# A fused hash attention and MoE kernel: score windows of one PSUM bank in a rotation of three, two output accumulators, a new plan and start fillers

## The chip, the cores and the metric

One core of a Trainium2 chip. The metric is the device time of one execution in microseconds (us). Times are medians over several executions; the span of a profile is 1.5 to 2 us less. The kernel before runs in 360 us.

PE is TensorE's matmuls and PEld its weight loads; ACT is ScalarE, DVE is VectorE, POOL is GpSimd. PSUM is the memory into which matmuls write. AV is the product of the exps of the scores with V. MoE is the name of the two last matmuls of the reference, with h * sigmoid(h) between them.

## The reference, cut to what matters

```python
def _attn_ref(q, k, v, proj):            # q, k, v: 4 x 8 x 768 x 64
    q_bits = (np.einsum('bhsd,dk->bhsk', q, proj) > 0)   # 6 bits; k_bits alike
    mask = q_bucket[:, :, :, None] == k_bucket[:, :, None, :]
    scores = np.where(mask, scale * np.matmul(q, k.transpose(0, 1, 3, 2)), -1e9)
    attn = softmax(scores)               # written out in the original
    return np.matmul(attn, v)

x = attn_out.transpose(0, 2, 1, 3).reshape(B * S, H * D)   # 3072 x 512
h = x @ w_in                             # 512 x 2048
return (h * sigmoid(h)) @ w_out          # 2048 x 512
```

There are 32 heads. A block of 768 rows of x needs all eight heads of its batch, so the MoE of batch b runs between the heads of batch b + 1. The first batch has no MoE work beside it, and the MoE of the last batch runs alone at the end.

## The kernel before

PSUM has eight banks. The general pool `m` has three, the scores `s` four (two tiles of 768 columns, each over two banks), the accumulator `o` one.

```python
def score(s):                            # one key tile of a head
    sp = ps.tile([P, S], F32, tag="s", name="s_ps", bufs=2)
    ks = t[rows, S + jt * P : S + (jt + 1) * P]
    for c0, c1 in ((0, 512), (512, S)):
        nc.tensor.matmul(sp[:, c0:c1], ks, t[rows, c0:c1], start=True, stop=True)
    u = upl.tile([P, S], F16, tag="u", name="u")
    nc.scalar.activation(out=u, in_=sp, func=AF.Exp, scale=ESC)

def av(s):
    if jt == 0:                          # a new head: start the accumulator
        o_ps[h] = ps.tile([P, NJ, E1], F32, tag="o", name="o_ps", bufs=1)
        nc.tensor.matmul(o_ps[h], dmat, vs[...].to_broadcast(...), start=True, stop=True)
    for t in range(NJ):                  # six matmuls of 65 columns
        nc.tensor.matmul(o_ps[h][:, t, :], u[:, t * P : (t + 1) * P], vv[:, jt, :], ...)
    if jt == NJ - 1:                     # head done: normalise on VectorE
        nc.vector.reciprocal(out=rec, in_=o[:, :, D])
        nc.vector.tensor_tensor(out=x_pr[p][...], in0=o[:, :, 0:D], in1=rec..., op=ALU.mult)
# ...
for s in range(NSTEP):
    for fn in at.pop(s, []): fn()        # planned units
    # ... n MoE units from the queue
    av(s)
    if s + 2 < NSTEP: score(s + 2)
```

The planned units are: `t_unit` (four f32 transposes of q or k, and a copy from PSUM), `cast_unit` (POOL, f16 copies of q and k), `proj_unit` (the six hash bits by matmul), `bits_unit` (VectorE writes bits below q and k, so that the score matmul masks by itself), `v_unit` (POOL) and `x_unit` (transpose of the normalised output).

The softmax here doesn't subtract the row's maximum and nothing guards it: scores larger than these inputs give would overflow.

Of the kernel before, what the change touches and what calls it, by code (L numbers as in the profile page):

```python
# [9 lines left out]
F32 = mybir.dt.float32  # L10
F16 = mybir.dt.float16
# [6 lines left out]
def kernel(  # L18
# [10 lines left out]
    nc = tc.nc  # L29
# [19 lines left out]
    vld = ctx.enter_context(tc.tile_pool(name="vld", bufs=4))  # L49
    t32 = ctx.enter_context(tc.tile_pool(name="t32", bufs=4))  # L50
    btp = ctx.enter_context(tc.tile_pool(name="btp", bufs=2))
    upl = ctx.enter_context(tc.tile_pool(name="upl", bufs=4))
    nrm = ctx.enter_context(tc.tile_pool(name="nrm", bufs=2))
    xpl = ctx.enter_context(tc.tile_pool(name="xpl", bufs=2))
    thp = ctx.enter_context(tc.tile_pool(name="thp", bufs=3))
# [10 lines left out]
    def load_qk(p):  # L66
        b, h0 = p // 4, 2 * (p % 4)
        for n, src in (("q", q), ("k", k)):
            t = ld.tile([P, NJ, 2, D], F32, tag=f"ld{n}", name=f"{n}_sb")
            nc.sync.dma_start(  # L70
                out=t, in_=src[b, h0 : h0 + 2].rearrange("h (p t) d -> p t h d", p=P))
            qk_sb[p, n] = t
# [15 lines left out]
    nc.vector.memset(dmat, DELTA)  # L88
    warm = cst.tile([P, 512], BF16, name="warm")
    nc.vector.memset(warm, 0.5)  # L90
    wps = ps.tile([P, 512], F32, tag="o", name="warm_ps", bufs=1)

    def warm_up(n):
        for _ in range(n):
# [47 lines left out]
    def load_w_in(dt):  # L142
        nc.gpsimd.dma_start(out=w_in16[dt], in_=moe_w_in[P * dt : P * (dt + 1), :])
# [9 lines left out]
    def t_unit(p, i, warm=0):  # L153
        if i == 0:
            qk32[p] = t32.tile([P, 2 * S], F32, tag="qk32", name="qk32")
        tp = ps.tile([P, 512], F32, tag="m", name="tp_ps", bufs=3)
        for j in range(4):
            n, t = divmod(4 * i + j, NJ)
            src = qk_sb[p, "qk"[n]]
            if t == 0 and n == 1:  # L160
                warm_up(warm)
            nc.tensor.transpose(tp[:, j * P : (j + 1) * P],  # L162
                                src[:, t].rearrange("p h d -> p (h d)"), ident)
        dst = qk32[p][:, 512 * i : 512 * (i + 1)]
        if p > 3 or p == 0 and i != 1:
            nc.scalar.copy(dst, tp)  # L166
        else:
            nc.vector.tensor_copy(out=dst, in_=tp)

    def cast_unit(p, par):  # L170
        sl = p % NSL
        dst, rows = ((QKA[sl], slice(0, 64)), (QKB[sl], slice(64, 128)))[par]
        nc.gpsimd.tensor_scalar(out=dst[rows, :], in0=qk32[p][rows, :],  # L173
                                scalar1=CS, scalar2=1.0,
                                op0=ALU.mult, op1=ALU.mult)

    def v_unit(p, heads=(0, 1)):
        for i in heads:
            h = 2 * p + i
            vv, vs = VV[h % NVS], VS[h % NVS]  # L180
            src = v_sb[p][:, i, :].rearrange("p (t d) -> p t d", d=D)
            nc.gpsimd.tensor_copy(out=vv[:, :, 0:D], in_=src)
            sa = nrm.tile([P, 3, D], F32, tag="vsa", name="vsa")
            nc.gpsimd.tensor_tensor(out=sa, in0=src[:, 0:3], in1=src[:, 3:6], op=ALU.add)  # L184
            sb = nrm.tile([P, D], F32, tag="vsb", name="vsb")
            nc.gpsimd.tensor_tensor(out=sb, in0=sa[:, 0], in1=sa[:, 1], op=ALU.add)
            nc.gpsimd.tensor_tensor(out=vs[:, 0:D], in0=sb, in1=sa[:, 2], op=ALU.add)
# [33 lines left out]
                nc.vector.tensor_copy(out=dst, in_=bits[pairs][r, :])  # L221


    st = {}
    ut = {}

    def score(s):
        h, jt = divmod(s, NJ)
        p, par = divmod(h, 2)
        t = QKA[p % NSL] if par == 0 else QKB[p % NSL]  # L230
        rows = slice(0, 65 + NBIT) if par == 0 else slice(0, P)
        sp = ps.tile([P, S], F32, tag="s", name="s_ps", bufs=2)
        ks = t[rows, S + jt * P : S + (jt + 1) * P]
        for c0, c1 in ((0, 512), (512, S)):
            nc.tensor.matmul(sp[:, c0:c1], ks, t[rows, c0:c1], start=True, stop=True)  # L235
        u = upl.tile([P, S], F16, tag="u", name="u")
        nc.scalar.activation(out=u, in_=sp, func=AF.Exp, scale=ESC)  # L237
        ut[s] = u

    o_ps = {}  # L240
    x_pr = {}

    def av(s):
        h, jt = divmod(s, NJ)
        vv, vs = VV[h % NVS], VS[h % NVS]
        if jt == 0:
            o_ps[h] = ps.tile([P, NJ, E1], F32, tag="o", name="o_ps", bufs=1)
            nc.tensor.matmul(o_ps[h], dmat, vs[:, None, :].to_broadcast([P, NJ, E1]),  # L248
                             start=True, stop=True)
        u = ut.pop(s)  # L250
        for t in range(NJ):
            nc.tensor.matmul(o_ps[h][:, t, :], u[:, t * P : (t + 1) * P], vv[:, jt, :],  # L252
                             start=False, stop=True,
                             skip_group_check=True)
        if jt == NJ - 1:
            o = o_ps.pop(h)
            p, par = divmod(h, 2)
            if par == 0:
                x_pr[p] = xpl.tile([P, NJ, P], F16, tag="xpr", name="x_pr")
            rec = nrm.tile([P, NJ], F32, tag="rec", name="rec")  # L260
            nc.vector.reciprocal(out=rec, in_=o[:, :, D])  # L261
            nc.vector.tensor_tensor(out=x_pr[p][:, :, par * D : (par + 1) * D],  # L262
                                    in0=o[:, :, 0:D],
                                    in1=rec[:, :, None].to_broadcast([P, NJ, D]),
                                    op=ALU.mult)
# [58 lines left out]


    NH = B * H
    NSTEP = NH * NJ
    QST = 4 * NJ

    t_unit(0, 0)  # L330
    t_unit(0, 1, warm=6)
    t_unit(0, 2)
    cast_unit(0, 0)
    v_unit(0, (0,))
    proj_unit(0)
    bits_unit((0,), 0, 0)
    cast_unit(0, 1)
    v_unit(0, (1,))
    bits_unit((0,), 0, 1)

    at = {}

    def plan(step, fn):
        at.setdefault(step, []).append(fn)


    for i in range(3):
        plan(1 + i, lambda i=i: t_unit(1, i))
    plan(3, lambda: cast_unit(1, 0))
    plan(3, lambda: cast_unit(1, 1))  # L350
    plan(5, lambda: proj_unit(1))
    plan(5, lambda: bits_unit((1,), 0, 0))
    plan(6, lambda: bits_unit((1,), 0, 1))
    plan(6, lambda: v_unit(1))
    for i in range(2):
        plan(0, lambda p=2 + i: load_qk(p))
    for i in range(2):
        plan(2 + i, lambda p=2 + i: load_v(p))

    for i in range(6):  # L360
        plan(8 + 2 * i, lambda i=i: t_unit(2 + i // 3, i % 3))
        if i % 3 == 2:
            for par in range(2):
                plan(8 + 2 * i, lambda p=2 + i // 3, par=par: cast_unit(p, par))
    plan(19, lambda: proj_unit(2, 3))
    for i in range(4):
        plan(19 + i, lambda i=i: bits_unit((2, 3), i // 2, i % 2))
    for i in range(2):
        plan(14 + i, lambda p=2 + i: v_unit(p))
    for dt in range(NDT):  # L370
        plan(8 + 4 * dt, lambda dt=dt: load_w_in(dt))
        plan(25 + 4 * dt, lambda dt=dt: load_w_out(dt))
    for i in range(2):
        plan(14 + i, lambda p=4 + i: load_qk(p))

    for Q in range(2, NQUAD):
        s0 = (Q - 1) * QST
        for i in range(6):
            plan(s0 + 2 * i, lambda Q=Q, i=i: t_unit(2 * Q + i // 3, i % 3))
            if i % 3 == 2:  # L380
                for par in range(2):
                    plan(s0 + 2 * i, lambda p=2 * Q + i // 3, par=par: cast_unit(p, par))
        plan(s0 + 13, lambda Q=Q: proj_unit(2 * Q, 2 * Q + 1))
        for i in range(4):
            plan(s0 + 14 + i,
                 lambda Q=Q, i=i: bits_unit((2 * Q, 2 * Q + 1), i // 2, i % 2))
        for i in range(2):
            plan(s0 + 1 + i, lambda p=2 * Q + i: load_v(p))
            plan(s0 + 16 + i, lambda p=2 * Q + i: v_unit(p))
            if Q + 1 < NQUAD:  # L390
                plan(s0 + 12 + i, lambda p=2 * Q + 2 + i: load_qk(p))
    for p in range(NPAIR):
        plan(12 * (p + 1) + 2, lambda p=p: x_unit(p))

    moeq = deque()
    score(0)
    score(1)
    for s in range(NSTEP):
        for fn in at.pop(s, []):
            fn()  # L400
        if s % 48 == 3 and s > 48:
            moeq.extend(moe_units(s // 48 - 1))
        keep = 3 if s >= NSTEP - 8 else 0
        left = 48 - s % 48
        n = -(-(len(moeq) - keep) // left) if len(moeq) > keep else 0
        for _ in range(n):
            moeq.popleft()()
        av(s)
        if s + 2 < NSTEP:
            score(s + 2)  # L410
    while moeq:
        moeq.popleft()()
    for s in sorted(at):
        for fn in at[s]:
            fn()
    for u in moe_units(B - 1):
        u()


# [1 line left out]
_INS = ['q', 'k', 'v', 'proj', 'moe_w_in', 'moe_w_out']  # L421
# [26 lines left out]
```

## Time and profile before

The span, cut at the first exp, at the first MoE matmul of three batches, and at the last AV matmuls (the prediction cuts up to 0.4 us elsewhere). Each busy time is of the stretch; the last column is the mean granted clock. This profile is of an execution of 361.78 us with a recorded clock of 0.976, which the record counts as slow. No fast execution of this kernel was profiled.

| stretch | us | PE busy | ACT busy | clock |
|---|---|---|---|---|
| start | 13.15 | 9.35 | 2.46 | 1.00 |
| first batch, attention alone | 62.3 | 52.9 | 43.5 | 0.86 |
| mixed 1, attention and MoE | 81.8 | 77.9 | 57.2 | 1.00 |
| mixed 2 | 81.8 | 77.9 | 57.1 | 1.00 |
| mixed 3 | 72.1 | 67.6 | 50.5 | 1.00 |
| MoE alone | 48.9 | 45.0 | 14.3 | 1.00 |

In the views below, a wait line names who waited, `<-` for whom, then us in total, times, and the longest. A line of the timeline gives start, us, engine, source line, operation, tiles, shapes and count; in brackets, the idle time just before and who ended it. Ends of matmuls are modelled.

Two lines of the page are of use beside those that the prediction shows: the granted clock in 40 slices of 9 us, in tenths, and the matmul that starts an accumulator, with busy time, mean ns, then idle before it and who ended most of that.

```profile
PEclk9789989699999999999999999999999999999999
L248 PE MATMUL o_ps<-vs,dmat 128*128 128x390 f16 x32 | 10.9, 341 | 19.0 <-DVE x_pr L262 16.8
```

The clock falls in the first 75 us alone. PE stood still for 19.0 us ahead of 32 short matmuls, 16.8 of it until a normalisation had read the one accumulator.

### The profile page before, as it was taken

The numbers are of one execution on the slowest core, as the hardware profiler recorded it, in microseconds if no ns is written. First come the engines' busy times: TensorE is split into PE (matmuls) and PEld (weight loads), VectorE is DVE, ScalarE is ACT, GpSimd is POOL, SyncE is SP. The second block draws the span as 40 slices with busy tenths as digits, with TensorE's granted clock in tenths as the row PEclk, the third lists the DMA queues.
The fourth block names the chain that finished last, engine by engine and source line by source line (L and its number), as shares of the span: only waits on it lengthen the run. The fifth ranks groups of instructions, "written<-read, shape, count | busy, mean of one in ns | idle before, by whom it ended". The sixth has DMA issues, their size and how long they took to land.

```text
span 360.0 us, 7115 instructions
## 1 busy us (share of the span) xinstructions
PE 330.6 (92%) x2893; PEld 195.7 (54%) x2893; DVE 162.4 (45%) x335; ACT 225.0 (63%) x327; POOL 111.9 (31%) x178
## 2 busy tenths in 40 slices
PE   7779798699989999999989999999989999999995
PEld 4446364365467664565457664555457555446542
DVE  4555615344584216245594116235584222277421
ACT  2348688598678664688678564588778465366200
POOL 5766968411820228002730229003640000000000
PEclk9789989699999999999999999999999999999999
DMA  8999999900000008397000009230000001000012
GB/s 185 237 240 251 237 183 219 231 6 0 2 2 1 31 29 182 84 213 169 2 0 3 29 31 188 76 118 2 1 3 0 31 31 58 32 29 2 29 60 87
DMA packets 60257, 29.83 MB, mean 83 GB/s; under 512 B 50496, under 2 KB 56640, under 8 KB 60224
## 3 DMA queue, kind: packets, MB, share of 16 engines
q1 hardware_dynamic: 57472, 25.17, 29.5%
q0 software_dynamic: 2752, 4.20, 6.7%
q8 instruction: 23, 0.38, 0.5%
q14 instruction: 10, 0.08, 0.1%
HBM read 27.27 MB, written 6.29 MB: 93 GB/s over the span
## 4 chain that ended last, share of the span: by engine, by line
PE 71%; DVE 16%; ACT 4%; issue 3%; POOL 3%; DMA 1%; ACTq 0%; POOLq 0%
PE o_ps L306 22%; PE h_ps L289 18%; PE s_ps L235 13%; PE o_ps L252 8%; DVE g L295 5%; PE tp_ps L162 4%; DVE x_pr L262 4%; PE bp_ps L201 3%; PE o_ps L248 3%; DVE qka L221 2%; ACT th L293 2%; ACT u L237 2%; DVE osb L311 1%; DVE qkb L218 1%; DMA q_sb<-in_q_dram 1%
## 5 line engine op out<-in xcount | busy, mean ns | idle before, releaser
L237 ACT ACTIVATE u<-s_ps 128x768 f16<-128x768 f32 x192 | 153.9, 812 | 82.7 <-PE s_ps L235 81.9
L306 PE MATMUL o_ps<-wout,g 128*128 128x512 f16 x384 | 94.5, 379 | 0.0
L289 PE MATMUL h_ps<-xT,win 128*128 128x512 f16 (+1 forms) x512 | 93.8, 326 | 0.3 <-DVE xT L274 0.3
L295 DVE SCALAR_TENSOR_TENSOR g<-th,h_ps 128x512 f16<-128x512 f32 x96 | 66.0, 687 | 49.5 <-ACT th L293 49.2
L252 PEld LDWEIGHTS <-u 128*128 128x128 f16 x1152 | 59.9, 100 | 40.0 <-ACT u L237 13.2
L252 PE MATMUL o_ps<-vv,u 128*128 128x65 f16 x1152 | 68.5, 197 | 2.6 <-ACT u L237 2.0
L293 ACT ACTIVATE th<-h_ps 128x512 f32<-128x512 f32 x96 | 57.3, 597 | 21.8 <-PE h_ps L289 19.2
L173 POOL TENSOR_SCALAR qka<-qk 64x1536 f16<-64x1536 f32 x16 | 23.4, 1462 | 145.3 <-ACT qk L166 137.6
L289 PEld LDWEIGHTS <-win 128*128 128x128 f16 x512 | 49.5, 98 | 31.1 <-issue 1.8
L306 PEld LDWEIGHTS <-g 128*128 128x128 f16 x384 | 37.0, 98 | 36.3 <-issue 0.8
L235 PE MATMUL s_ps<-qka 71*128 71x512 f16 x192 | 48.9, 337 | 1.9 <-DVE qka L221 1.9
L235 PE MATMUL s_ps<-qkb 128*128 128x512 f16 x192 | 48.2, 333 | 0.0
L311 DVE TENSOR_SCALAR osb<-o_ps 128x512 f32<-128x512 f32 x24 | 16.6, 692 | 63.9 <-PE o_ps L306 63.9
L248 PE MATMUL o_ps<-vs,dmat 128*128 128x390 f16 x32 | 10.9, 341 | 19.0 <-DVE x_pr L262 16.8
L166 ACT COPY qk<-tp_ps 128x512 f32<-128x512 f32 x38 | 22.2, 584 | 6.0 <-PE tp_ps L162 6.0
L173 POOL TENSOR_SCALAR qkb<-qk 64x1536 f16<-64x1536 f32 x16 | 23.5, 1469 | 1.3
L274 DVE COPY xT<-xt_ps 128x768 f16<-128x768 f16 x16 | 8.9, 556 | 23.1 <-PE xt_ps L272 23.0
L184 POOL TENSOR_TENSOR vsa<-v_sb 128x192 f32<-128x192 f32 x32 | 19.3, 604 | 0.0
L248 PEld LDWEIGHTS <-dmat 128*128 128x128 bf16 x32 | 3.1, 96 | 29.3 <-issue 14.9
L261 DVE RECIPROCAL rec<-o_ps 128x6 f32<-128x6 f32 x32 | 6.1, 190 | 27.7 <-PE o_ps L252 27.6
L262 DVE TENSOR_TENSOR x_pr<-o_ps,rec 128x384 f16<-128x384 f32 x32 | 17.8, 557 | 1.1
L206 DVE TENSOR_SCALAR bits<-bp_ps,sc 128x512 f16<-128x512 f32 (+3 forms) x18 | 11.3, 671 | 14.7 <-PE bp_ps L201 14.7
(43 smaller groups left out, 212.4 us busy)
## 6 DMA issues: line engine op xcount, KB each, us to landing
q_sb<-in_q_dram SPq DMA_DIRECT2D x16, 384.0 KB, 7.1
k_sb<-in_k_dram SPq DMA_DIRECT2D x16, 384.0 KB, 7.0
v_sb<-in_v_dram SPq DMA_DIRECT2D x16, 384.0 KB, 5.5
out_dram<-osb SPq DMA_DIRECT2D x24, 256.0 KB, 2.0
win<-in_moe_w_in_dram POOLq DMA_DIRECT2D x4, 512.0 KB, 6.9
wout<-in_moe_w_out_dram POOLq DMA_DIRECT2D x4, 512.0 KB, 10.1
pw<-in_proj_dram POOLq DMA_DIRECT2D x2, 1.5 KB, 4.6
```

Of the source, the lines that this page charges most:

```text
L166: nc.scalar.copy(dst, tp)
L173: nc.gpsimd.tensor_scalar(out=dst[rows, :], in0=qk32[p][rows, :], scalar1=CS, scalar2=1.0, op0=ALU.mult, op1=ALU.mult)
L235: nc.tensor.matmul(sp[:, c0:c1], ks, t[rows, c0:c1], start=True, stop=True)
L237: nc.scalar.activation(out=u, in_=sp, func=AF.Exp, scale=ESC)
L248: nc.tensor.matmul(o_ps[h], dmat, vs[:, None, :].to_broadcast([P, NJ, E1]), start=True, stop=True)
L252: nc.tensor.matmul(o_ps[h][:, t, :], u[:, t * P : (t + 1) * P], vv[:, jt, :], start=False, stop=True, skip_group_check=True)
L262: nc.vector.tensor_tensor(out=x_pr[p][:, :, par * D : (par + 1) * D], in0=o[:, :, 0:D], in1=rec[:, :, None].to_broadcast([P, NJ, D]), op=A ...
L289: nc.tensor.matmul(hp[:, j, :], w_in16[dt][:, ft * P : (ft + 1) * P], xT[4 * b + dt][:, c0 : c0 + n], start=(dt == 0), stop=(dt == NDT - 1))
L293: nc.scalar.activation(out=th, in_=hp, func=AF.Tanh, scale=0.5)
L295: nc.vector.scalar_tensor_tensor(out=g[ci][:, grp * f : (grp + 1) * f, :], in0=th, scalar=1.0, in1=hp, op0=ALU.add, op1=ALU.mult)
L306: nc.tensor.matmul(o2[tt], g[ci][:, ft, ct * P : (ct + 1) * P], w_out16[:, ft, :], start=(ft == 0), stop=(ft == NFT - 1))
L311: nc.vector.tensor_scalar(out=osb, in0=o2[tt], scalar1=0.5, scalar2=None, op0=ALU.mult)
```

## The change

The same matmul columns, cut otherwise: a head has nine score windows of 512 columns (the middle one of three holds the 256-column rests of two key tiles), each in one bank. Three of them rotate, and the bank that this frees is a second accumulator. The plan is rewritten in windows, with the projections behind a head's end; the start has more filler matmuls and a cast on ScalarE in place of POOL.

```diff
+    LEAD = 3
-        sp = ps.tile([P, S], F32, tag="s", name="s_ps", bufs=2)
+        sp = ps.tile([P, 512], F32, tag="s", name="s_ps", bufs=LEAD)
-        for c0, c1 in ((0, 512), (512, S)):
-            nc.tensor.matmul(sp[:, c0:c1], ks, t[rows, c0:c1], start=True, stop=True)
+        for jt, c0, n, o0 in pts:
+            nc.tensor.matmul(sp[:, o0 : o0 + n], t[rows, S + jt * P : S + (jt + 1) * P],
+                             t[rows, c0 : c0 + n], start=True, stop=True)
-            o_ps[h] = ps.tile([P, NJ, E1], F32, tag="o", name="o_ps", bufs=1)
+            o_ps[h] = ps.tile([P, NJ, E1], F32, tag="o", name="o_ps", bufs=2)
 ...
-    t_unit(0, 1, warm=6)
+    t_unit(0, 1, warm=4)
     t_unit(0, 2)
+    warm_up(3)
     cast_unit(0, 0)
-    v_unit(0, (0,))
+    cast_unit(0, 1)
+    v_unit(0)
     proj_unit(0)
+    warm_up(9)
 ...
-    plan(5, lambda: proj_unit(1))
+    plan(9, lambda: proj_unit(1))
 ...
-        plan(s0 + 13, lambda Q=Q: proj_unit(2 * Q, 2 * Q + 1))
+        plan(w0 + 19, lambda Q=Q: proj_unit(2 * Q, 2 * Q + 1))
 ...
-        if s + 2 < NSTEP:
-            score(s + 2)
+        if w + LEAD < NW:
+            score(w + LEAD)
```

MoE units go into the first two of three windows. The SBUF pool of the exps goes from four tiles of 768 columns to six of 512, which are the same columns. The rest of the diff converts step numbers to window numbers.

More of the change, by code (lines that the diff above doesn't have):

```diff
@@ L51 @@
     btp = ctx.enter_context(tc.tile_pool(name="btp", bufs=2))
-    upl = ctx.enter_context(tc.tile_pool(name="upl", bufs=4))
+    upl = ctx.enter_context(tc.tile_pool(name="upl", bufs=6))
     nrm = ctx.enter_context(tc.tile_pool(name="nrm", bufs=2))
@@ L90 @@
     nc.vector.memset(warm, 0.5)
-    wps = ps.tile([P, 512], F32, tag="o", name="warm_ps", bufs=1)
+    wps = ps.tile([P, 512], F32, tag="o", name="warm_ps", bufs=2)
     def warm_up(n):
@@ L172, in cast_unit @@
         dst, rows = ((QKA[sl], slice(0, 64)), (QKB[sl], slice(64, 128)))[par]
+        if p == 0 and par == 1:
+            nc.scalar.mul(dst[rows, :], qk32[p][rows, :], CS)
+            return
         nc.gpsimd.tensor_scalar(out=dst[rows, :], in0=qk32[p][rows, :],
@@ L221, in bits_unit, with parts, score @@
                 nc.vector.tensor_copy(out=dst, in_=bits[pairs][r, :])
-    st = {}
+    NU = 9
+    LEAD = 3
     ut = {}
-    def score(s):
-        h, jt = divmod(s, NJ)
+    def parts(w):
+        h, r = divmod(w, NU)
+        jp, j = divmod(r, 3)
+        if j == 1:
+            return h, [(2 * jp, 512, 256, 0), (2 * jp + 1, 512, 256, 256)]
+        return h, [(2 * jp + j // 2, 0, 512, 0)]
+    def score(w):
+        h, pts = parts(w)
         p, par = divmod(h, 2)
@@ L231, in score, with av @@
         rows = slice(0, 65 + NBIT) if par == 0 else slice(0, P)
-        sp = ps.tile([P, S], F32, tag="s", name="s_ps", bufs=2)
-        ks = t[rows, S + jt * P : S + (jt + 1) * P]
-        for c0, c1 in ((0, 512), (512, S)):
-            nc.tensor.matmul(sp[:, c0:c1], ks, t[rows, c0:c1], start=True, stop=True)
-        u = upl.tile([P, S], F16, tag="u", name="u")
+        sp = ps.tile([P, 512], F32, tag="s", name="s_ps", bufs=LEAD)
+        for jt, c0, n, o0 in pts:
+            nc.tensor.matmul(sp[:, o0 : o0 + n], t[rows, S + jt * P : S + (jt + 1) * P],
+                             t[rows, c0 : c0 + n], start=True, stop=True)
+        u = upl.tile([P, 512], F16, tag="u", name="u")
         nc.scalar.activation(out=u, in_=sp, func=AF.Exp, scale=ESC)
-        ut[s] = u
+        ut[w] = u
     o_ps = {}
     x_pr = {}
-    def av(s):
-        h, jt = divmod(s, NJ)
+    def av(w):
+        h, pts = parts(w)
         vv, vs = VV[h % NVS], VS[h % NVS]
-        if jt == 0:
-            o_ps[h] = ps.tile([P, NJ, E1], F32, tag="o", name="o_ps", bufs=1)
+        if w % NU == 0:
+            o_ps[h] = ps.tile([P, NJ, E1], F32, tag="o", name="o_ps", bufs=2)
             nc.tensor.matmul(o_ps[h], dmat, vs[:, None, :].to_broadcast([P, NJ, E1]),
                              start=True, stop=True)
-        u = ut.pop(s)
-        for t in range(NJ):
-            nc.tensor.matmul(o_ps[h][:, t, :], u[:, t * P : (t + 1) * P], vv[:, jt, :],
-                             start=False, stop=True,
-                             skip_group_check=True)
-        if jt == NJ - 1:
+        u = ut.pop(w)
+        for jt, c0, n, o0 in pts:
+            for i in range(n // P):
+                nc.tensor.matmul(o_ps[h][:, c0 // P + i, :],
+                                 u[:, o0 + i * P : o0 + (i + 1) * P], vv[:, jt, :],
+                                 start=False, stop=True, skip_group_check=True)
+        if w % NU == NU - 1:
             o = o_ps.pop(h)
@@ L326, with plan @@
     NH = B * H
-    NSTEP = NH * NJ
-    QST = 4 * NJ
+    NW = NH * NU
+    BST = 8 * NU
+    QST = 4 * NU
     t_unit(0, 0)
-    t_unit(0, 1, warm=6)
+    t_unit(0, 1, warm=4)
     t_unit(0, 2)
+    warm_up(3)
     cast_unit(0, 0)
-    v_unit(0, (0,))
+    cast_unit(0, 1)
+    v_unit(0)
     proj_unit(0)
+    warm_up(9)
     bits_unit((0,), 0, 0)
-    cast_unit(0, 1)
-    v_unit(0, (1,))
     bits_unit((0,), 0, 1)
     at = {}
-    def plan(step, fn):
-        at.setdefault(step, []).append(fn)
+    def plan(w, fn):
+        at.setdefault(w, []).append(fn)
@@ L347 @@
     for i in range(3):
-        plan(1 + i, lambda i=i: t_unit(1, i))
-    plan(3, lambda: cast_unit(1, 0))
-    plan(3, lambda: cast_unit(1, 1))
-    plan(5, lambda: proj_unit(1))
-    plan(5, lambda: bits_unit((1,), 0, 0))
-    plan(6, lambda: bits_unit((1,), 0, 1))
-    plan(6, lambda: v_unit(1))
+        plan(1 + 2 * i, lambda i=i: t_unit(1, i))
+    plan(5, lambda: cast_unit(1, 0))
+    plan(5, lambda: cast_unit(1, 1))
+    plan(9, lambda: proj_unit(1))
+    plan(9, lambda: v_unit(1))
     for i in range(2):
+        plan(10 + i, lambda i=i: bits_unit((1,), 0, i))
@@ L356 @@
         plan(0, lambda p=2 + i: load_qk(p))
-    for i in range(2):
-        plan(2 + i, lambda p=2 + i: load_v(p))
+        plan(3 + i, lambda p=2 + i: load_v(p))
     for i in range(6):
-        plan(8 + 2 * i, lambda i=i: t_unit(2 + i // 3, i % 3))
+        plan(12 + 3 * i, lambda i=i: t_unit(2 + i // 3, i % 3))
         if i % 3 == 2:
             for par in range(2):
-                plan(8 + 2 * i, lambda p=2 + i // 3, par=par: cast_unit(p, par))
-    plan(19, lambda: proj_unit(2, 3))
+                plan(12 + 3 * i, lambda p=2 + i // 3, par=par: cast_unit(p, par))
@@ L366 @@
+    plan(28, lambda: proj_unit(2, 3))
     for i in range(4):
-        plan(19 + i, lambda i=i: bits_unit((2, 3), i // 2, i % 2))
+        plan(29 + i, lambda i=i: bits_unit((2, 3), i // 2, i % 2))
     for i in range(2):
-        plan(14 + i, lambda p=2 + i: v_unit(p))
+        plan(21 + i, lambda p=2 + i: v_unit(p))
+        plan(21 + i, lambda p=4 + i: load_qk(p))
     for dt in range(NDT):
-        plan(8 + 4 * dt, lambda dt=dt: load_w_in(dt))
-        plan(25 + 4 * dt, lambda dt=dt: load_w_out(dt))
@@ L373 @@
-    for i in range(2):
-        plan(14 + i, lambda p=4 + i: load_qk(p))
+        plan(12 + 6 * dt, lambda dt=dt: load_w_in(dt))
+        plan(38 + 6 * dt, lambda dt=dt: load_w_out(dt))
     for Q in range(2, NQUAD):
-        s0 = (Q - 1) * QST
+        w0 = (Q - 1) * QST
         for i in range(6):
-            plan(s0 + 2 * i, lambda Q=Q, i=i: t_unit(2 * Q + i // 3, i % 3))
+            plan(w0 + 3 * i, lambda Q=Q, i=i: t_unit(2 * Q + i // 3, i % 3))
             if i % 3 == 2:
                 for par in range(2):
-                    plan(s0 + 2 * i, lambda p=2 * Q + i // 3, par=par: cast_unit(p, par))
-        plan(s0 + 13, lambda Q=Q: proj_unit(2 * Q, 2 * Q + 1))
+                    plan(w0 + 3 * i, lambda p=2 * Q + i // 3, par=par: cast_unit(p, par))
@@ L384 @@
+        plan(w0 + 19, lambda Q=Q: proj_unit(2 * Q, 2 * Q + 1))
         for i in range(4):
-            plan(s0 + 14 + i,
+            plan(w0 + 20 + i,
                  lambda Q=Q, i=i: bits_unit((2 * Q, 2 * Q + 1), i // 2, i % 2))
         for i in range(2):
-            plan(s0 + 1 + i, lambda p=2 * Q + i: load_v(p))
-            plan(s0 + 16 + i, lambda p=2 * Q + i: v_unit(p))
+            plan(w0 + 1 + i, lambda p=2 * Q + i: load_v(p))
+            plan(w0 + 24 + i, lambda p=2 * Q + i: v_unit(p))
@@ L390 @@
             if Q + 1 < NQUAD:
-                plan(s0 + 12 + i, lambda p=2 * Q + 2 + i: load_qk(p))
+                plan(w0 + 18 + i, lambda p=2 * Q + 2 + i: load_qk(p))
     for p in range(NPAIR):
-        plan(12 * (p + 1) + 2, lambda p=p: x_unit(p))
+        plan(2 * NU * (p + 1) + 3, lambda p=p: x_unit(p))
     moeq = deque()
-    score(0)
-    score(1)
-    for s in range(NSTEP):
-        for fn in at.pop(s, []):
-            fn()
-        if s % 48 == 3 and s > 48:
-            moeq.extend(moe_units(s // 48 - 1))
-        keep = 3 if s >= NSTEP - 8 else 0
-        left = 48 - s % 48
+    for w in range(LEAD):
+        score(w)
@@ L405 @@
+    for w in range(NW):
+        for fn in at.pop(w, []):
+            fn()
+        if w % BST == 4 and w > BST:
+            moeq.extend(moe_units(w // BST - 1))
+        keep = 3 if w >= NW - 12 else 0
+        left = BST - w % BST
         n = -(-(len(moeq) - keep) // left) if len(moeq) > keep else 0
+        if w % 3 == 2 and n == 1 and len(moeq) - keep < left:
+            n = 0
         for _ in range(n):
             moeq.popleft()()
-        av(s)
-        if s + 2 < NSTEP:
-            score(s + 2)
+        av(w)
+        if w + LEAD < NW:
+            score(w + LEAD)
@@ L411 @@
     while moeq:
         moeq.popleft()()
-    for s in sorted(at):
-        for fn in at[s]:
+    for w in sorted(at):
+        for fn in at[w]:
             fn()
```

## The prediction

> **What bounds the kernel now.** I read the page's busy table first (PE 92% busy, ACT 63%), then cut the span at the first exp (13.15 us), the starts of the MoE matmuls of the first three batches (75.6, 157.4, 239.2) and the last attention step (311.5). The view of these stretches, with busy time of PE, PEld, DVE, ACT, POOL, then the clock, DMA share and GB/s:
>
> ```profile
> 0.00:13.15 13.15, 9.35 (x36) 4.41 (x37) 6.53 (x50) 2.46 (x3) 8.25 (x16) 1.00 1.01 208
> 13.15:75.60 62.45, 53.02 (x552) 32.19 (x551) 28.68 (x56) 43.66 (x60) 40.15 (x63) 0.86 1.08 214
> 75.60:157.40 81.80, 77.92 (x722) 47.63 (x720) 37.07 (x71) 57.17 (x85) 25.41 (x40) 1.00 0.17 45
> 157.40:239.20 81.80, 77.93 (x722) 47.62 (x720) 37.05 (x71) 57.10 (x85) 25.40 (x40) 1.00 0.34 79
> 239.20:311.50 72.30, 67.81 (x626) 40.65 (x625) 30.56 (x58) 50.30 (x73) 12.74 (x20) 1.00 0.07 24
> 311.50:360.00 48.50, 44.56 (x242) 23.23 (x240) 22.56 (x34) 14.34 (x24) 0.00 (x0) 1.00 0.10 39
> ```
>
> The reader is to see two kinds of stretch. The first batch (62.45 us) holds attention alone: PE idles 9.4 us and its clock is 0.86. In the three mixed stretches PE is idle only 3.9 to 4.5 us each, 12.2 us together; they are PE-bound. The last stretch is MoE alone.
>
> A busy PE is not a PE at its peak, so I took the true cost of each piece from start-to-start times in a mixed stretch, PE then ACT:
>
> ```profile
> 251.87 1.03 PE L289 MATMUL h_ps<-xT,win 128*128 128x512 f16 x4
> 252.73 0.35 PE L252 MATMUL o_ps<-vv,u 128*128 128x65 f16 x6
> 252.92 0.49 PE L235 MATMUL s_ps<-qkb 128*128 128x512 f16 x2
> 253.24 0.60 PE L162 MATMUL tp_ps<-ident,k_sb 128*128 128x128 f32 x4
> 253.68 1.03 PE L289 MATMUL h_ps<-xT,win 128*128 128x512 f16 x4
> ```
> ```profile
> 252.93 0.60 ACT L293 ACTIVATE th<-h_ps 128x512 f32<-128x512 f32 x1
> 253.44 0.81 ACT L237 ACTIVATE u<-s_ps 128x768 f16<-128x768 f32 x1
> 254.15 0.58 ACT L166 COPY qk<-tp_ps 128x512 f32<-128x512 f32 x1
> ```
>
> So PE needs 0.86 us for four MoE matmuls, 0.19 for six AV matmuls (32 ns each), 0.32 for the scores of one key tile, 0.44 for four f32 transposes; ACT needs 0.51 for 512 columns and 0.71 for 768. The first batch at these prices: 48 steps of 0.51 = 24.5, transposes of pairs 1 to 5 (15 x 0.44) = 6.6, projections about 3.9, x transposes 1.0, accumulator starts 8 x 0.165 = 1.3: 37 us of PE work in 62.45. What fills the rest are the waits of PE, then of its weight loads, in that stretch:
>
> ```profile
> PE o_ps L248 <- DVE x_pr L262: 5.4, 7, 2.9
> PE o_ps L248 <- POOL vsb L186: 2.2, 1, 2.2
> PE o_ps L252 <- ACT u L237: 1.2, 4, 0.5
> ```
> ```profile
> PEld L252 <- ACT u L237: 11.9, 26, 0.8
> ```
>
> The second fence is waiting that the modelled ends of matmuls hide. The half clock adds up to 0.14 x 62.45 = 8.7 us. From 75.6 to 311.5 there is one main wait of PE, 11.4 us, on the single accumulator:
>
> ```profile
> PE o_ps L248 <- DVE x_pr L262: 11.4, 17, 1.5
> ```
>
> **What the Trainium skill says.** "PSUM — Partial Sum Buffer", Specifications: eight banks of 512 fp32 values. A 768-column score tile thus takes two banks; before, scores hold four banks, `m` three, the accumulator one. The change makes it three, three, two. "Perfetto Trace Analysis", Optimizing Tensor Performance, Matmuls: independent groups should rotate through different banks, so that evacuation overlaps the next group; the 17 waits on x_pr are that lack. "ScalarE: Activation LUTs", What ACT_TABLE_LOAD costs: 186 ns + 0.833 ns a column, back-to-back overlap about 93 ns. That gives 520 ns for 512 columns; the trace has 510, and I use 510. "TensorE: Matmul & The Clock Gate", Part 1: the clock halves after an idle window of about 3.4 us, and matmuls start N / 2.4 GHz + 2.5 ns apart; 512 + 256 columns make 0.325, the trace has 0.32. The clock of 0.50 in 15 to 20 us and 65 to 70 us agrees with the first: both follow long stalls.
>
> **The change, part by part.** Scores: the same matmuls and columns, in 288 windows of 512 instead of 192 of 768. PE cost unchanged. ACT pays one fixed part more per three windows: 3 x 0.51 = 1.53 against 2 x 0.71 = 1.42, so 0.11 x 96 = +10.6 us of ACT over the kernel (about 245 - 250 us busy by the modelled durations), all off the path where PE binds.
>
> Rotation of three instead of two: the lookahead in columns is 1,536 both times. But the loop differs. Before, after exp(s), PE does AV 0.19 + scores 0.32 + end about 0.17 + signals about 0.06 = 0.74 before ACT can take exp(s+2), while ACT has only exp(s+1), 0.71, to do; any transpose unit (0.44) in between is fully exposed. After, PE needs 0.13 + 0.21 + 0.23 = 0.57 while ACT has two windows, 1.02: slack 0.45, just a transpose unit. So the first batch moves from a PE-ACT ping-pong to an ACT bound. It runs to window 76: 76 x 0.51 = 38.8, ACT copies of pairs 4 and 5 (6 x 0.5) 3.0, three projections of 0.8 to 1.4 us exposed by about 0.9 each, 2.7, and 2.5 allowed for late bits, casts or loads: 47 us. PE does 37 of these, so it stays warm. 62.45 - 47 = 15.5 us saved. This includes the clock's 8.7 and the accumulator's 5.4; they are not added again.
>
> Second accumulator: in the mixed stretches the 11.4 us go, with perhaps 0.16 hidden behind each of 17 waits, 2.7 more. PE work there cannot go under about 77 of 81.8 us per full batch (45 steps at 0.51, 48 units at 0.86, transposes, projections). I take 10 us of the 12.2 visible.
>
> Plan and start: normalisations come before the projection's bit copies in VectorE's queue, which takes away stalls like the 2.9 us one at 63 us. The QKB cast of pair 0 moves from POOL (1.47 us) to ACT, idle at that time; V of head 1 is ready earlier. The first chain (loads, transposes, copies, POOL cast, bits) is unchanged. Nine fillers of 0.22 after the projection last 2 us, in the 2.0 us until bits are ready (10.3 to 12.6 us); two fewer ahead of k's transposes can save 0.4, three before the projection can cost 0.2. Start: -0.3 us. At the end nothing changes.
>
> Sum: 360.5 - 15.5 - 10 - 0.3 = 334.7, say 335 us.
>
> **The rivals.** (1) ACT becomes the bound also in the mixed stretches. While the first MoE matmul's tanh run, three windows ask of ACT 3 x 0.51 + 2 x 0.51 + a copy 0.5 = 3.05 us, of PE 3 x 0.34 + 2 x 0.86 + 0.44 = 3.18. ACT at 96% in these parts, some 25 us per batch, speaks for small waits; the mm2 half (1.53 against 2.74) speaks against. If it bites, 1 to 2 us per batch come back: 340. (2) The first batch meets POOL or the loads. POOL needs 6.5 us a pair (two casts 1.47, V work 3.6) plus 0.6 for each weight load, and pairs will be used up every 18 x 0.55 = 10 us instead of 13: it fits, but its queue is strict. DMA runs at 214 GB/s there; eight pairs (9.4 MB) and w_in (4.2 MB) take 57 to 63 us, and the first MoE batch would now start near 60. The issues for pair 7 are out at 36 us already, which speaks against. If it bites, 4 to 6 us return: 340. (3) The x_pr wait was only the last of several, and another (bits, V sums, xT) takes its place: half of both gains lost, 347. That PE busy equals the summed work in the mixed stretches (77.9 against 77) speaks against: there was nothing else behind that wait.
>
> **Range and chances.** Rivals 1 and 2 together give about 345; the best case, ACT saturated with no exposure (first batch 43) and all visible idle gone, about 328. So 328 to 345. A gain of 2% needs 353 us; to miss it, both main mechanisms must give under a third. Faster 0.95, within 2% 0.04, slower 0.01.
>
> **What would show it.** The wait of PE on x_pr should vanish or fall under 2 us, the idle of PE in the mixed stretches under 2 us per batch, the first MoE matmul should start at 58 to 62 us, the clock of the first batch be 0.97 or more, and exps in it stand 0.51 apart. Wrong it would be if waits of AV's weight loads on ACT appeared in the mixed stretches (rival 1), if score matmuls waited for casts, bits or loads (rival 2), or if the first batch still took over 55 us.

## The result, and the profile after

The changed kernel takes 331.84 us (331.66 to 332.09, four runs), the kernel before 360.14 us in the same session (357.79 to 361.89, four runs). The ratio is 0.9218, with a 95% interval of 0.9164 to 0.9273. Ratios are those over fast runs; they are not quite the ratio of the medians.

The same cuts in the changed kernel; columns are the stretch, its length, busy time of PE, PEld, DVE, ACT and POOL, then clock, DMA share and GB/s:

```profile
0.00:12.40 12.40, 10.41 (x46) 5.10 (x47) 6.41 (x50) 3.93 (x4) 8.23 (x16) 1.00 1.00 206
12.40:59.36 46.96, 46.28 (x549) 29.21 (x548) 27.52 (x56) 42.46 (x86) 38.83 (x62) 1.00 1.16 225
59.36:136.81 77.45, 77.31 (x722) 48.58 (x720) 37.92 (x71) 57.59 (x110) 25.73 (x40) 1.00 0.33 81
136.81:214.26 77.45, 77.31 (x722) 48.59 (x721) 37.90 (x71) 57.51 (x110) 25.74 (x40) 1.00 0.35 83
214.26:281.20 66.94, 66.80 (x621) 41.18 (x620) 31.30 (x57) 50.78 (x96) 12.76 (x20) 1.00 0.08 27
281.20:330.20 49.00, 45.02 (x251) 23.57 (x249) 22.55 (x34) 14.33 (x24) 0.00 (x0) 1.00 0.12 44
```

| stretch | before | after | difference |
|---|---|---|---|
| start | 13.15 | 12.40 | -0.75 |
| first batch | 62.3 | 47.0 | -15.3 |
| three mixed | 235.6 | 221.8 | -13.8 |
| MoE alone | 48.9 | 49.0 | +0.1 |

The column before is of a slow execution (361.78 us, with a recorded clock of 0.976; no fast execution of this kernel was profiled), so the gain of the first batch is an upper figure.

PE has next to no idle time left in the mixed stretches (77.31 of 77.45). The longest waits of PE, then those of its weight loads in the first batch, and the clock:

```profile
PE warm_ps L95 <- DVE pw L101: 1.6, 1, 1.6
PE tp_ps L162 <- DMA q_sb<-in_q_dram: 0.4, 1, 0.4
PE o_ps L266 <- ACT u L250: 0.3, 1, 0.3
```
```profile
PEld L266 <- ACT u L250: 10.1, 35, 0.7
```
```profile
PEclk9999999999999999999999999999999999999999
```

The wait on x_pr, 16.8 us before, is gone from the list. What remains in the first batch is that AV's weight loads, whose weights are the exps, wait for ACT. ACT itself, in the first batch:

```profile
31.86 4.03 ACT L250 ACTIVATE u<-s_ps 128x512 f16<-128x512 f32 x8 [1.65 <-PE s_ps L247]
35.69 0.68 ACT L166 COPY qk<-tp_ps 128x512 f32<-128x512 f32 x1
36.15 1.69 ACT L250 ACTIVATE u<-s_ps 128x512 f16<-128x512 f32 x3
```

Eight exps in 4.03 us, the last of 0.60, start (4.03 - 0.60) / 7 = 0.49 us apart. Then three exps and one copy come back to back. The 1.65 us in brackets is ACT waiting for scores while PE did a projection.

### The profile page after: what moved, and what is told of

Same layout as the page of the kernel before. It is cut to its first block, busy times and chain, and to the rows that moved or that the text cites. A ratio compares the mean times of both kernels' runs of the same rounds, so it can differ in the third digit from the quotient of the medians.

```text
span 330.2 us, 7269 instructions
## 1 busy us (share of the span) xinstructions
PE 323.1 (98%) x2903; PEld 196.2 (59%) x2903; DVE 163.6 (50%) x335; ACT 226.6 (69%) x424; POOL 111.3 (34%) x177
## 4 chain that ended last, share of the span: by engine, by line
PE 90%; DVE 5%; ACT 2%; DMA 1%; issue 0%; ACTq 0%
PE o_ps L320 25%; PE h_ps L303 24%; PE s_ps L247 17%; PE o_ps L266 11%; PE tp_ps L162 6%; PE bp_ps L204 4%; DVE qka L224 2%; PE o_ps L261 2%; DMA q_sb<-in_q_dram 1%; PE xt_ps L286 1%; ACT u L250 1%; PE warm_ps L95 1%; DVE g L309 1%; DVE qkb L221 1%; DVE xT L288 1%; DVE qkb L224 1%
## 5 line engine op out<-in xcount | busy, mean ns | idle before, releaser
L250 ACT ACTIVATE u<-s_ps 128x512 f16<-128x512 f32 x288 | 160.2, 622 | 48.8 <-PE s_ps L247 48.4
L266 PEld LDWEIGHTS <-u 128*128 128x128 f16 x1152 | 69.9, 97 | 42.4 <-ACT u L250 10.1
L309 DVE SCALAR_TENSOR_TENSOR g<-th,h_ps 128x512 f16<-128x512 f32 x96 | 65.7, 686 | 47.5 <-ACT th L307 47.3
L266 PE MATMUL o_ps<-vv,u 128*128 128x65 f16 x1152 | 82.4, 194 | 0.6 <-ACT u L250 0.3
L247 PE MATMUL s_ps<-qkb 128*128 128x512 f16 x192 | 53.1, 326 | 0.0
L247 PE MATMUL s_ps<-qka 71*128 71x512 f16 x192 | 52.7, 327 | 0.0
L166 ACT COPY qk<-tp_ps 128x512 f32<-128x512 f32 x38 | 24.5, 645 | 5.4 <-PE tp_ps L162 5.4
L276 DVE TENSOR_TENSOR x_pr<-o_ps,rec 128x384 f16<-128x384 f32 x32 | 17.8, 557 | 1.1
L185 POOL CAST vv<-v_sb 128x384 f16<-128x384 f32 x32 | 17.8, 555 | 0.5
L224 DVE COPY qka<-bits 13x768 f16<-13x768 f16 x32 | 16.4, 514 | 0.7
L162 PE MATMUL tp_ps<-ident,q_sb 128*128 128x128 f32 x96 | 16.0, 279 | 0.4 <-DMA q_sb<-in_q_dram 0.4
L247 PEld LDWEIGHTS <-qka 71*128 71x128 f16 x192 | 15.5, 97 | 0.5 <-POOL vsb L189 0.3
```

What stands on the lines that cost most here:

```text
L162: nc.tensor.transpose(tp[:, j * P : (j + 1) * P], src[:, t].rearrange("p h d -> p (h d)"), ident)
L166: nc.scalar.copy(dst, tp)
L224: nc.vector.tensor_copy(out=dst, in_=bits[pairs][r, :])
L247: nc.tensor.matmul(sp[:, o0 : o0 + n], t[rows, S + jt * P : S + (jt + 1) * P], t[rows, c0 : c0 + n], start=True, stop=True)
L266: nc.tensor.matmul(o_ps[h][:, c0 // P + i, :], u[:, o0 + i * P : o0 + (i + 1) * P], vv[:, jt, :], start=False, stop=True, skip_group_check ...
L309: nc.vector.scalar_tensor_tensor(out=g[ci][:, grp * f : (grp + 1) * f, :], in0=th, scalar=1.0, in1=hp, op0=ALU.add, op1=ALU.mult)
```

## The experiments

Each run was timed in rounds with the kernel before; its medians in the three sessions are 360.0, 360.0 and 359.8 us, so sessions can be compared (e9, e11, e12 and e13 ran on another chip than the other experiments). All results were correct.

### The two uses of the freed banks: four runs

**e1_one_acc** takes the second accumulator away and leaves a bank unused.

```diff
-    wps = ps.tile([P, 512], F32, tag="o", name="warm_ps", bufs=2)
+    wps = ps.tile([P, 512], F32, tag="o", name="warm_ps", bufs=1)
-            o_ps[h] = ps.tile([P, NJ, E1], F32, tag="o", name="o_ps", bufs=2)
+            o_ps[h] = ps.tile([P, NJ, E1], F32, tag="o", name="o_ps", bufs=1)
```

> The changed kernel with one output accumulator instead of two; the bank so freed stays unused. My theory: the second accumulator alone gives back what the mixed stretches lost (235.9 us of stretch before, 222.1 after, so 13.8) and some 3 to 5 us of the first batch: 347 to 351 us, the waits of PE on x_pr back at 11 to 17 us in the trace. Rival (the rotation of score banks does the work, the accumulator's wait would be hidden by three windows of lookahead): 332 to 338 us.

350.31 us (348.86 to 350.98), ratio to before 0.9745. The mixed stretches took 232.8 us (11.0 more than the changed kernel), the first batch 53.0 (6.0 more). The wait is back, and the clock falls again (the second line is the first batch, clock 0.97):

```profile
PE o_ps L261 <- DVE x_pr L276: 15.0, 21, 2.3
```
```profile
12.28:65.32 53.04, 47.02 (x550) 30.20 (x548) 26.92 (x56) 43.42 (x86) 38.82 (x62) 0.97 1.12 227
```

So the accumulator is worth 18.5 us as the last part added. The rival, that three windows of lookahead hide the wait, is out.

**e2_two_score_banks** keeps two accumulators and rotates two score banks.

```diff
-    LEAD = 3
+    LEAD = 2
```

> The changed kernel with two score banks in rotation instead of three (lookahead two windows), two accumulators kept. My theory: the first batch goes back to a ping-pong of PE and ACT, 76 windows of about 0.57 us plus 15 transposes of 0.44 exposed plus the same 8 us of copies and projections, about 58 us instead of 46.8; the mixed stretches lose about 1 us each: 343 to 348 us. Rival (first batch was held up by accumulator, clock and bits, not by the ping-pong): 332 to 336 us.

343.99 us (343.60 to 344.44), ratio 0.9564. The first batch took 57.3 us, 10.3 more; the mixed stretches 223.3, 1.5 more. The waits of PE and of its weight loads:

```profile
PE o_ps L266 <- ACT u L250: 9.1, 26, 0.5
```
```profile
PEld L266 <- ACT u L250: 23.1, 48, 0.8
```

Where these were 0.3 and 10.1 us with three banks, they are 9.1 and 23.1 with two. Around the first batch ACT waited for scores 38 times, 13.7 us in all, against 5 times and 6.5 us with three: PE and ACT take turns. The clock of the first batch is 1.00 here, so the 10.3 us are waiting alone.

**e3_two_banks_one_acc** undoes both (the edits of e1 and e2 together).

> Both undone: two score banks, one accumulator, but windows of 512, plan and fillers of the change kept. If the two parts are independent, the losses of the two runs above add up: 360 to 366 us, no faster than the kernel before, since ACT pays 0.11 us more per three windows. Rival (plan and fillers bring a good part of the gain): 345 to 352 us.

361.99 us (361.81 to 363.36), ratio 1.0072. From 331.84 the loss is 30.2; the two losses alone add to 18.5 + 12.2 = 30.6. The parts are additive within half a microsecond, and the first theory holds: without the banks, smaller windows, plan and fillers do not beat the kernel before.

**e4_four_banks_one_acc** gives the eighth bank to a fourth score window.

```diff
-    LEAD = 3
+    LEAD = 4
```
(and one accumulator, as in e1)

> The eighth bank given to a fourth score bank instead of a second accumulator. My theory: no extra score bank can hide the wait of the next accumulation on x_pr[...]: within 3 us of the run with one accumulator and three score banks, so 345 to 351 us, with the mixed stretches as long as there. Rival (more lookahead of scores covers any wait): 332 to 338 us.

349.22 us (347.66 to 349.48), ratio 0.9700. Its mixed stretches sum to 232.6 us, against 232.8 with three score banks and one accumulator. The wait is as long as the 15.0 us of e1:

```profile
PE o_ps L261 <- DVE x_pr L276: 15.2, 18, 3.2
```

The same bank is worth 18.5 us as an accumulator and 1.1 us as a fourth score window (the ranges of e1 and e4 overlap, so this may be nothing). More lookahead does not hide the wait: PE ran nothing past the waiting matmul, for up to 3.2 us.

### The start and the clock: three runs

**e5_no_fill** has the fillers of the kernel before in the changed kernel.

```diff
-    t_unit(0, 1, warm=4)
+    t_unit(0, 1, warm=6)
-    warm_up(3)
-    warm_up(9)
```

> The changed kernel with the filler matmuls of the kernel before (6 in the first transposes, none around the first projection). My theory: PE idles about 2 us before the first scores, the clock falls to half for some 4 to 5 us as it did from 15 to 20 us before; PE is near its bound in the first batch, so 1.5 to 2.5 us are lost: 333.3 to 334.5 us. Rival (first batch is ACT-bound, half the clock is hidden): 331.5 to 332.3 us.

Six runs: 334.70, 334.11, 334.03, 334.06, 331.98, 331.93, median 334.04, ratio 0.9276. The median lies in the theory's band, but two runs lost nothing. Their recorded clock is 0.998 and 0.999, that of the four others 0.993. PE at the first scores of the profiled run, and three lines further on:

```profile
13.11 0.81 PE L247 MATMUL s_ps<-qka 71*128 71x512 f16 x4 [1.91 <-DVE qka L224]
...
15.52 0.43 PE L266 MATMUL o_ps<-vv,u 128*128 128x65 f16 x4
...
17.24 0.63 PE L162 MATMUL tp_ps<-ident,k_sb 128*128 128x128 f32 x2
17.67 0.35 PE L266 MATMUL o_ps<-vv,u 128*128 128x65 f16 x4
17.85 0.38 PE L247 MATMUL s_ps<-qka 71*128 71x512 f16 x1
18.07 0.29 PE L266 MATMUL o_ps<-vv,u 128*128 128x65 f16 x4
```

After 1.91 us without work the AV groups take 0.43 us and the transposes 0.63, until about 17.7 us, when AV is back at 0.29; the first batch's clock is 0.96. With the fillers all four runs lie within 0.43 us. So the fillers bring about 2.1 us in the runs in which the clock would have fallen, and a steady time.

The first batch of this profile is 48.61 us, 1.65 more than in the changed kernel. The clock was at half for 3.4 us, which loses 1.7 us of matmul work, so nearly all of it came through. The rival (ACT bounds the first batch and hides this) is out for that part of it.

**e6_before_fill** puts the fillers alone into the kernel before.

```diff
-    t_unit(0, 1, warm=6)
+    t_unit(0, 1, warm=4)
     t_unit(0, 2)
+    warm_up(3)
 ...
     proj_unit(0)
+    warm_up(9)
```

> The kernel before with the fillers of the changed one and nothing else. My theory: the first fall of the clock goes, the two at 45 to 50 and 65 to 70 us stay, since they follow stalls in mid-batch: 1.5 to 3 us faster than before, about 357 to 359 us. Rival (the clock's falls hang together, and the warm start heals them all): 351 to 353 us.

357.13 us (356.40 to 358.01), ratio 0.9946 (0.9880 to 1.0012). The median is 2.9 us lower, as expected, but the interval includes 1, for the kernel before spreads over 4.6 us in that session. The first batch is 58.6 us in the profile instead of 62.3 in the slow execution of the kernel before, and its clock 0.94 instead of 0.86. Part of the clock's falls remain, but not those that the theory names. The first fall and that of 45 to 50 us are gone, although PE waits 1.07 us at the same place as before. That of 65 to 70 us is there (63.7 to 67.1), and a new one came from 22.7 to 26.1 us, behind a wait of 2.34 us on V work of POOL that lowered nothing in the kernel before (2.22 us).

This run gives e3 another reading. With the same fillers, the old windows of 768 (357.13) are 4.9 us faster than two windows of 512 (361.99). The smaller windows do not pay by themselves. But the 4.9 us are not the price of the cut alone: e3 holds two score banks instead of four, so 1,024 columns of lookahead instead of 1,536, and has the new plan. Its loss is in the first batch (65.0 us against 58.6); its mixed stretches are 1.5 us shorter (234.2 against 235.7). No run prices the cut apart.

**e11_cast_pool** has the cast of pair 0 back on POOL and the V work around it.

```diff
-        if p == 0 and par == 1:
-            nc.scalar.mul(dst[rows, :], qk32[p][rows, :], CS)
-            return
```
(and the order of V, cast and bits at the start as before)

> The changed kernel with the second cast of pair 0 back on POOL and the V work of the two heads around it, as before. My theory: it was not in the first chain; scores of head 1 need the cast at window 6, some 3 us after the first, POOL has it done about 14.3 us: 331.8 to 333.5 us. Rival (it sets the start): 334 us or more.

332.58 us (331.66 to 333.37), ratio 0.9251. That is 0.7 us above the changed kernel, with overlapping ranges: in the expected band, and too small to say more. All stretches after the first exp are the same within 0.1 us. The first exp came at 13.07 us, 0.67 later than in the changed kernel. This lag was there before a cast could matter: k's transposes began at 7.79 us instead of 7.12, and from them to the first scores both took 4.87 us. In the ten profiles with the cast on ACT and the fillers the first exp lies between 12.10 and 12.97. So the cast was not in the first chain.

### The plan and what is left in the first batch: four runs

**e7_old_order** plans projections and bit copies where the kernel before had them.

```diff
-    plan(9, lambda: proj_unit(1))
+    plan(8, lambda: proj_unit(1))
-        plan(10 + i, lambda i=i: bits_unit((1,), 0, i))
+        plan(8 + i, lambda i=i: bits_unit((1,), 0, i))
-        plan(29 + i, ...bits_unit((2, 3), i // 2, i % 2))
+        plan((28, 30, 31, 33)[i], ...)
-            plan(w0 + 20 + i,
+            plan(w0 + (21, 23, 24, 26)[i],
```

> The changed kernel with projections and bit copies planned where the kernel before had them, in window numbers (first projection ahead of the first normalisation, last bit copies ahead of the last one of a quad). My theory: with two accumulators a late normalisation blocks nobody for a whole head, so the order is worth little: 331.5 to 333.5 us. Rival (order is what removed the stalls): 336 us or more.

330.71 us (330.66 to 331.59), ratio 0.9214. That is below the expected band: the old order is 1.1 us better, not a little worse. The three mixed stretches sum to 221.0 us instead of 221.8, and PE is busy in the whole of them. The new order thus brings nothing once there are two accumulators. Whether the order ahead of the normalisation or the wider spacing of the bit copies makes the 1.1 us was not tried apart.

**e8_copies_dve** moves six PSUM copies of the first batch from ACT to VectorE.

```diff
-        if p > 3 or p == 0 and i != 1:
+        if p > 5 or p == 0 and i != 1:
             nc.scalar.copy(dst, tp)
```

> The changed kernel with the PSUM copies of the transposes of pairs 4 and 5 on VectorE instead of ScalarE. My theory says that ACT bounds the first batch: 6 copies of about 0.5 us go from it, VectorE (26 of 42 us busy there) takes them, 2 to 3 us gained: 328.8 to 330 us. Rival (PE bounds it too, or VectorE's queue gets in the way): 331.5 us or more.

330.31 us (330.02 to 330.81), ratio 0.9197. The gain is 1.5 us, a little short of the band. The first batch in it:

```profile
12.88:58.04 45.16, 44.84 (x549) 29.63 (x548) 32.27 (x62) 39.91 (x80) 38.83 (x62) 1.00 1.15 220
```

It is 1.8 us shorter, with six ACT instructions less (x80 against x86) and all mixed stretches unchanged. So ACT does set much of the first batch's pace, but not all: of the 3.0 us of copies (6 x 0.5) 1.2 did not come back, and ACT's waits for scores there went from 6.5 to 7.0 us. This is the lowest median of all runs.

**e9_split_proj** plans the two column chunks of each projection in neighbouring windows.

```diff
-    plan(9, lambda: proj_unit(1))
+    for i in range(2):
+        plan(9 + i, lambda i=i: proj_unit(1, half=(i,)))
```
(all projections alike; `half` picks the chunk)

> The changed kernel with each projection split into its two column chunks, planned in neighbouring windows, so that PE is not taken from the scores for 1.43 us at a stretch. My theory: three projections leave ACT without work in the first batch by about 1.2 to 1.6 us each; two shorter pieces (0.95 and 0.48) leave it idle about half of that: 1.5 to 2.5 us gained, 329.3 to 330.3 us, all in the first batch. Rival (the bits come later by a window and hold up scores, or PE bounds the batch): 331.5 us or more.

333.17 us (332.81 to 333.67), ratio 0.9272: 1.3 us slower, so the theory missed. ACT around the same projection as above, now split:

```profile
31.78 0.60 ACT L253 ACTIVATE u<-s_ps 128x512 f16<-128x512 f32 x1 [1.22 <-PE s_ps L250]
32.80 3.54 ACT L253 ACTIVATE u<-s_ps 128x512 f16<-128x512 f32 x7 [0.42 <-PE s_ps L250]
```

ACT waits 1.22 + 0.42 = 1.64 us where it waited 1.65. A likely reading is that the first chunk empties the lookahead and the second comes before it has filled again; no run tests it. Nothing is gained there, and the first two mixed stretches are 77.7 us instead of 77.45. The first batch is 0.5 us longer although ACT's waits for scores are 6.5 us in both; why is open.

**e12_all** joins the edits of e8 and e9 and the spread of e7.

> A better version, put together from what the runs show: copies of pairs 4 and 5 on VectorE (gained 1.5 us), bit copies spread as in the run with the old order (gained 1.1), and split projections (expected 1.5 to 2.5). If they add up: 327 to 328.5 us. Rival (they relieve the same wait): 329.5 to 330.5 us.

330.85 us (330.39 to 331.31), ratio 0.9207: neither of the two numbers, since the split, which was counted as a gain, is a loss. It does not beat e8. The edits of e7 and e8 without the split were not run together.

### One more bank for scores, one less for the rest

**e13_lead4_m2** gives a fourth bank to the scores out of the general pool, with split projections (a whole one would want two general banks at once).

```diff
-    LEAD = 3
+    LEAD = 4
-        tp = ps.tile([P, 512], F32, tag="m", name="tp_ps", bufs=3)
+        tp = ps.tile([P, 512], F32, tag="m", name="tp_ps", bufs=2)
```
(all five tiles of the pool alike)

> Split projections, four score banks, two accumulators, two general banks in place of three. My theory: a fourth window gives ACT 0.5 us more of work ahead, first batch 1 to 2 us shorter than with split projections alone; but the MoE's first product with two banks must wait for tanh and product (0.86 + 0.2 + 0.6 + 0.7 us against two turns of 1.2), so its half of the mixed stretches gets 2 to 6 us longer each: 335 to 345 us. Rival (two banks are enough there): 327 to 329 us.

357.46 us (357.45 to 357.56), ratio 0.9948. The direction is as expected, the size is not. The first batch is 1.0 us shorter than in e9 (46.5 against 47.5). The mixed stretches are 6.8, 6.7 and 3.7 us longer, and the last stretch, which the expectation forgot, is 57.6 us instead of 48.9. The longest waits of PE and of its weight loads:

```profile
PE h_ps L306 <- DVE g L312: 10.5, 26, 0.5
PE h_ps L306 <- DVE xT L291: 3.7, 4, 1.1
```
```profile
PEld L306 <- issue: 25.2, 38, 1.3
```

With two banks the MoE's first product waits for VectorE to finish with the last but one. The third general bank is worth more than any fourth for the scores.

## Why the prediction was right

**The sum.** 335 was predicted, 331.84 came; the range of 328 to 345 holds it. The largest error is one term, the accumulator below. A second one partly cancels it: the stretches before are from a slow execution. The two profiles differ by 29.8 us (360.0 and 330.2), the medians by 28.3, while the prediction took its savings from that profile off a median of 360.5. The other stretches have a full clock in both, so the 1.5 us most likely lie in the first batch, whose gain against the median would be nearer to 13.8 than to 15.3 us (an estimate from these differences; no run shows it). All five signs that the prediction named came: no wait on x_pr, 0.14 us of idle PE in each mixed stretch, the first MoE matmul at 59.36 us, a clock of 1.00, and exps about 0.51 us apart.

**First batch.** The prediction said 47 us, ACT-bound; it took 47.0. Its reason holds for most of the stretch: with the third bank taken away (e2) it becomes 57.3 with a full clock, and with six copies taken from ACT (e8) it becomes 45.2. It does not hold throughout: six copies of 0.5 us gave 1.8 us, not 3.0, and in e5 a slower PE cost nearly its full loss between 14.4 and 17.8 us, where the transposes of pair 1 fall. That 47 agrees so closely with 47.0 is partly luck, for two terms were off against each other. An exp in a run starts 0.49 (above) to 0.52 us after the last (twelve in 6.36 us, the last of 0.60); the latter makes 76 x 0.52 = 39.5, not 38.8. The waits of ACT for scores after the first exp were 1.22 + 0.22 + 1.65 + 1.07 = 4.2 us, mainly behind projections, where 2.7 for projections and 2.5 for late bits, casts and loads had been allowed. The spacing fits the page that the prediction cites, "ScalarE: Activation LUTs", What ACT_TABLE_LOAD costs: 520 ns is the estimate from its figures for 512 columns. In the profile after, PE has no wait for casts, bits or loads in this stretch, so the second rival did not occur.

**Second accumulator.** This is the term that was mis-sized: 10 us taken, 13.8 measured in the mixed stretches. In the same cuts before, PE was idle there for 81.8 + 81.8 + 72.1 - 77.9 - 77.9 - 67.6 = 12.3 us; after, for 0.4. The other 2 us lay behind the modelled ends of matmuls, and shrank its busy time from 223.4 to 221.4 (it is 223.6 again in e1). The prediction had named both (12.2 visible, up to 2.7 hidden) and took 10, without saying why. Its first rival, ACT at 96%, would have taken some back; it did not occur: in the mixed stretches no weight load waits on ACT. Not all 13.8 are the accumulator's alone. Taking it away (e1) costs 11.0 there, taking the third score bank away (e2) 1.5; with both undone (e3) they are still 1.4 us shorter than before. (The prediction's floor of 77 us for PE stands, but a full batch has 48 steps, eight heads of six, not 45; with 48 its prices come to about 77.)

**ACT.** 10.6 us more of ACT, or about 245 to 250 busy, was too much: its busy time went from 225.0 to 226.6 us, since exps that overlap are counted once. This cost lay off the path, as it was said, so the sum did not feel it.

**Clock.** It was said to follow from the stalls and not to be counted again. The profile after has 1.00 everywhere, and it falls again where long stalls are brought back: 0.96 without fillers, 0.97 with one accumulator. The clock of 1.00 in e2 shows the converse: waits of at most 0.8 us each, though 23 us of them in sum at the weight loads, did not lower it. The wide spread of the kernel before goes with the clock: its fastest execution (356.48 us) has a recorded clock of 0.995, those of 362 us have 0.976.

One reading was wrong: the falls do not agree with an idle window of 3.4 us. The waits of PE at the falls of the kernel before are 1.90, 1.07 and 2.94 us long. Nor does the length of a pause decide alone. In e4 the clock went to half at the first of these pauses (36.6 to 43.4 us) and not at the second:

```profile
37.03 0.48 PE L261 MATMUL o_ps<-vs,dmat 128*128 128x390 f16 x1 [1.72 <-DVE x_pr L276]
58.97 0.34 PE L261 MATMUL o_ps<-vs,dmat 128*128 128x390 f16 x1 [3.16 <-DVE x_pr L276]
```

What decides stays open.

**Start.** -0.3 was said, -0.75 is in the profile. From k's transposes to the first scores both kernels took 4.87 us (7.76 to 12.63 and 7.12 to 11.99), and so did e5 and e11. So the fillers around the projection cost nothing, where 0.2 had been allowed, and the cast gains nothing. The difference arose ahead of k's transposes, where two fillers fewer can save 0.4, and in the first window, which is smaller. As the first exp moves by nearly 0.9 us between profiles with the same fillers and cast, the size cannot be read closer.

**Plan.** The prediction put down part of the first batch to normalisations ahead of bit copies. This step was not needed: e7 shows that with two accumulators the old order does no harm.

**Third rival** (another wait takes the accumulator's place): the list of PE's waits after holds nothing above 0.4 us past the start, so no.

## What to carry to other kernels

Here PE waited for a consumer to release a buffer, and a second buffer of that kind helped where more lookahead in another queue did not: the same bank was worth 18.5 us in one place and 1.1 in the other. Count where each PSUM bank works, and try a costlier cut (512 instead of 768 columns) if it frees one; e3 shows that the cut without the use of the banks brings nothing. For the size of a gain, name the idle time and the busy time that exceeds the start-to-start sum apart (12.2 and up to 2.7 us here, against 13.8 gained), and give a reason for every allowance.

## What the Trainium skill lacked or had wrong

- "TensorE: Matmul & The Clock Gate", Part 1, gives an idle window of about 3.4 us for the clock's fall, and calls the window free-running. The lengths agree: every half-clock stretch in the first batches of these profiles lasts 3.4 or 6.8 us. The pause does not: 1.07 us (the kernel before, slow execution) and 1.72 us (e4) without matmuls came with half speed, 1.91 us in four of the six runs of e5 by their times and clocks, while 2.22 us (the kernel before) and 3.16 us (e4) did not.
- "Perfetto Trace Analysis", Optimizing Tensor Performance, Matmuls, says to rotate groups through banks, but no page says how to weigh the uses of a bank. Here: second accumulator 18.5 us, third score window 12.2, fourth score window beside one accumulator 1.1 (within the spread); and a fourth score window at the cost of the third general bank, -24.3 (e13 against e9).
- "Perfetto Trace Analysis", Identifying the Most-Contended Engine, warns of matmul busy time. The case bears it out (a group of six AV matmuls shows 0.35 us and costs 0.19), but the page does not say that the hidden waits stand with the weight loads: 10.1 us there against 0.3 at the matmuls.
